# The second MoE product of units 4 to 7 as seven half products

## The chip, the cores and the metric

One Trainium2 chip, one of its cores. The metric is the device time of one execution in microseconds; each kernel's time is the median of several executions. TensorE (PE) multiplies and loads weights (PEld), VectorE (DVE), ScalarE (ACT) and GpSimd (POOL) compute on tiles, and SyncE (SP) issues most transfers.

## The reference, cut to what matters

```python
# attention: batch 4, 8 heads, sequence 768, head dimension 64
k_sum = k.reshape(B, H, nb, 32, D).max(axis=3); v_sum = v.reshape(B, H, nb, 32, D).mean(axis=3)
scores = concat(where(|i - j| < 16, q k^T / sqrt(D), -1e9), q k_sum^T / sqrt(D) + log(32))
a = softmax(scores); attn = a @ concat(v, v_sum)
x = attn.transpose(0, 2, 1, 3).reshape(3072, 512)
# MoE
h = x @ w_in          # 3072 x 512 by 512 x 2048
g = h - tanh(h)
y = g @ w_out         # 3072 x 2048 by 2048 x 512
```

## The kernel before

The 3072 tokens are cut into eight units of 384 (half a sequence each), the 2048 hidden columns into 16 slices f of 128. For a unit the attention gives x transposed; a slice of the first product ("in") gives 128 hidden columns x 384 tokens in a PSUM bank; three ScalarE passes and one multiplication turn it into g (`moe_act_small`); the second product ("out", `moe_out`) adds g of that slice times a slice of `w_out` to three banks of 128 tokens x 512 columns, `pY0` to `pY2`.

To keep fp32 accuracy in a fast format every operand is split into a high and a low part, and a product is three matmuls: high x high, high x low, low x high. Those parts of g are made by `moe_split` (tiles gh and gl).

Units 2 to 7 are taken in pairs (2,3), (4,5), (6,7): their first product is already done as seven products of halves instead of eight (`moe_in_seven`). It needs sums of quarters of `w_in`, which `make_sums` computes once and stores in device memory (`scr`, 16 and more stores); `load_sums` brings them back for each pair into one of three buffers `wraw`. A group g of 0 to 7 gives four g-tiles: slices g and g + 8 of both units. `x_operands` makes the sums of the x quarters. The second product of all units is the plain one; `store_y` scales a bank into an SBUF tile on ScalarE and stores it.

Nothing is emitted as it is written: `do`, `either` and `dma` add tasks to a plan, with what they read and write. Then `follow` walks the written list `ORDER` of all 3628 tasks and emits them so; `ON` has a letter per task that picks the engine where there is a choice (D, A, P for VectorE, ScalarE, GpSimd, S for SP's queue, T for TensorE), `FILL` the number of small matmuls on the identity that are put ahead of a task to keep the clock up. So the order on each engine and on each queue is fixed by these lists. All instructions bear line 56, that of the helper that emits them, so groups are told apart by their tiles' names.

At the end `seen`, the largest sum of squares of h, decides whether a second, general version of the program runs; with these inputs it does not.

Of the kernel before, what the change touches and what calls it, by code (L numbers as in the profile page):

```python
# [21 lines left out]
RAWB = 3  # L22
# [7 lines left out]


FILL = {125: 18, 154: 12, 158: 2, 190: 14, 188: 6, 286: 2}
ON = 'PPAPAPPDDPPPPSSSSAASADSSSSDASSSDDASSSSSSSSSSSSSSSSASSDASASDSAASDDDSSSSSSSSSSSSDDDDSADDDSDDDDSDDDDSADDDSDDDDSADDDSADDDTAAAASSSTADDASSSTDDDDDDAAAAAADDDAAAPATATATATADDDDDDAAAAAAPDAAADAATDTATDTATDDDDDDAAAAAADDADAADPTATDTATADDDDDDAAAAAADDDADDDATATATATATTTTADAAAPSASSDTTTTDDAAAPSSSSSSSSSSSSSSTDDDDDDAAAAAADDDAPADATATATATADDDDDDDAAAAAADDPPAAAATATATATADTTTADTADAAAPSSSSTAAAATTTADTADAAAPSSSSDSSSSDDASSSSDSSSSDTTTADSDDDDTADAAAPSASSDTTTADSADDDTADAAAPAPSSSSSSSSSSSSSSTDDDDDDAAAAAADDAAADAPTATATATADDDDDDDAAAAAADDAADAAATATATATADSADDDAPTTTSDDDDTADAAADAPSSSSTAAAASADDDADTTTSADDDTADAAADADSADDDADTTTSADDDTADAAADADSADDDADTTTSADDDTADAAADADSADDDADTTTSADDDTADAAADADSADDDADTTTSADDDTADAAADAPSSSSSSSSSSSSSSTDDDDDDAAAAAAPDDDDDAAAAAATATATATADDDDDDAAAAAADDDDDDADAAAATATATATASADDDADTTTSADDDTADAAAPADSDDDDADTTTSDDDDTADAAADADSDDDDADTTTSADDDTADAAADADSADDDADTTTSADDDTADAAAPADSDDDDADTTTTAAADDDSSSSSSSSSSSSSSTDDDDDDAAAAAADDPDDDAAADAPTATATATADDDDDDAAAAAADDDDDDAAAAAATATATATASDDDDADTTTASASASTAAADADSSSSDSSSSDDASSSSDSSSSDTTTTAAADADSPSPSPSPTTTTAAADAPTTTTAAADAPTTTTAAADSSSSDDDDDDADSADSADSSSSSSSSSSSSSSTDDDDDDAAAAAAPDDDDDAAAAAATATATATADDDDDDAAAAAADDDDDDAAAAAATATATATATTTTAAADSSSSDDDDDPADSADSADTATTTTAAADSSSSDDPDDDADSADSADTTTTAAADSSSSDDDDDDADSADSAPTTTTAAADSSSSDDDDDDADSADSADSSSSSSSSSSSSSSTDDDDDDAAAAAADDPDDDAAAAAATATATDTADDDDDDAAAAAADDDDDDAAAAAATATATATATTTTAAADSSSSDDDDDDADSADSADTTTTAAADSSSSDDDDDDADSADSADSPSPSPSPTTTTAAADSSSSDDDDDDADSADSADTTTTAAADADTTTTAAADADTTTTAAADADTASSSSDSSSSDDPSSSSDSSSSDTTTADADADADADADDDDDDDDDADADADADADAPADADSSSTTADTATTADSTATDAAADADTTTASASAAAAADDPTTTSSSTTDDTATTDDSTATDAAADDPSSSSSSSSSSSSSSTDDDDDDAAAAAADDDDDDDDADAPTDTATDTDDDDDDDAAAAAADDPDDDDAPPAPTATDTDTATTTAAADDPTTTSSSTTADTDTTADSTDTDAAAPADTTTAAADADTTTSSSTTDDTDTTDDSTATDAAADADTTTAAAPDPTTTSSSTTDDTDTTDDSTATDAAADADTTTAAADDPSSSSSSSSSSSSSSTDDDDDDAAAAAADDDDDDDDPPAATDTDTATADDDDDDAAAAAADDPDDDAPDDDPTATATDTDTTTSSSTTDDTATTADSTDTDAAADAPSSSSDSSSSDDASSSSDSSSSDTTTAAADDDSPSPSPSPTTTSSSTTDDTDTTADSTATDAAADDDTTTAAAPDDTTTSSSTTDDTATTDDSTATDAAADDDTTTAAADDPTATTTAAADDDTTTASAAASAAADDDSSSSSSSSSSSSSSTDDDDDDAAAAAADDDDPDPPDPDPTATATATADDDDDDAAAAAADDDDDDDAPDADTDTDTDTDTTTAAADDDTTTAAAPDDTTTAAADDDTTTAAADDDTTTAAADADTTTAAADADTTTAAADDPSSSSSSSSSSSSSSTDDDDDDAAAAAADDDDDDDPDDDPTATDTATDDDDDDDAAAAAAPDDDDDAAPPAPTATATDTATTTAAADADSPSPSPSPTTTAAADADTTTAAADAPTTTAAADDDTTTAAADADTATTTAAADDPTTTAAADADSSSSDSSSSDDDSSSSDSSSSDTTTDPAPAPADADADPDDPDDDDADADDDDDADADDDADSSSTTADTATTADSTATDAAAPADTTTASAAASAAAPAPTTTSSSTTADTDTTADSTDTDAAADDDSSSSSSSSSSSSSSTDDDDDDAAAAAAPDDDDDDAPDPPTATDTATADDDDDDAAAAAAPDDDDDDPPAPPTATDTDTATTTAAAPAPTTTSSSTTDDTDTTADSTATDAAAPAPTTTAAAPDDTTTSSSTTDDTATTADSTATDAAADAPTTTAAADDDTTTSSSTTADTATTADSTDTDAAAPDPTTTAAAPDPSSSSSSSSSSSSSSTDDDDDDAAAAAADDDDPDPPADDATATATDTADDDDDDAAAAAAPDDDPDPDADPATDTDTDTDTTTSSSTTDDTDTTADSTATDAAAPAPSSSSDSSSSDDASSSSDSSSSDTTTAAADDDTTTSSSTTADTDTTADSTDTDAAAPADTTTAAAPDDTTTSSSTTDDTATTADSTATDAAAPDDTTTAAADAPTTTAAAPDDTTTASASASAAAPDDSSSSSSSSSSSSSSTDDDDDDAAAAAADDDDPDDDAPPPTDTDTATDDDDDDDAAAAAAPDDDDDAPDAAPTATATATATTTAAADDDTTTAAADDPTTTAAADAPTTTAAAPADTTTAAADDDTTTAAAPDDTTTAAAPDDSSSSSSSSSSSSSSTDDDDDDAAAAAADDPDDDPAPAADTDTDTATADDDDDDAAAAAADDDDDDDPDAPATDTATATATTTAAAPDDTTTAAADDPTTTAAAPDDTTTAAADADTTTAAADDDTTTAAADADTTTAAAPDDTTTADAPDDADADADDDDDPDDDADDDDDDPADADADADSSSTTDDTATTADSTDTDAAAPADTTTASASAAAAADAPTTTSSSTTDDTATTADSTDTDAAAPDPTTTAAADAPTTTSSSTTADTDTTDDSTATDAAADDDTTTAAADADTTTSSSTTDDTATTDDSTATDAAAPAPTTTAAADADTTTSSSTTDDTDTTDDSTDTDAAAPADTTTAAAPDDTTTSSSTTDDTATTADSTDTDAAADDDTTTAAADADTTTSSSTTADTDTTDDSTDTDAAAPAPTTTAAADAPTTTSSSTTADTDTTADSTATDAAAPDDTTTAAADDPTTTAAAPDDTTTASAAAAAAADDDTTTAAADADTTTAAADDDTTTAAADDDTTTAAADDDTTTAAADDDTTTAAADDDTTTAAADDPTTTAAADDDTTTAAADDDTTTAAADDDTTTAAADDPTTTAAAPAPTTTAAADDDTTTAAADDDTTTDDTTTAAASAASADTD'


SIGNED = set()

SLACK = 2.0

EITHER_QUEUE = {"y store"}
# [4 lines left out]
class Engine:  # L48


    def __init__(self, tc, engine):
        self._tc, self._engine = tc, engine

    def __getattr__(self, name):
        op = getattr(self._engine, name)
        return lambda *args, **kwargs: self._tc.keep_in_program_order(op(*args, **kwargs))  # L56


class Task:
    __slots__ = ("issue", "ahead", "index", "costs", "go", "after", "order", "level", "count", "ready", "next", "start", "engine", "cost", "place", "out", "banks", "behind", "moves", "kind", "name")  # L60

HELD = {"w shift", "w low", "w sign", "w low part", "w low part 2", "w high part", "w high part 2", "w scale", "normal", "g high", "g low", "g", "cube", "big", "top pre", "k move", "sum guard", "s whole", "s mix", "s high", "s low", "x mix", "x high", "x low"}
# [24 lines left out]
class Plan:  # L89
# [20 lines left out]
    def add(self, kind, costs, go, r=(), w=()):  # L110
# [15 lines left out]
        for base in dict.fromkeys(key[0] for key in (*r, *w)):  # L126
# [15 lines left out]
            self.touch.setdefault(base, []).append(t)  # L142
        t.after.discard(t)
        t.order.discard(t)
        t.order -= t.after
        return t

    def follow(self, idle):

        tasks = [self.tasks[n] for n in ORDER]  # L150
        free = dict.fromkeys((PE, DVE, ACT, POOL, SP), 0.65)
        dma, held, left = 0.0, {DVE: 0.0, POOL: 0.0}, 0.0
        clock, used, seen, done = Clock(), {}, {}, []
        spot, rest, lanes = 0, self.fill, [0.0] * 8
        for t in tasks:
            e = next(iter(t.costs)) if len(t.costs) == 1 else {"D": DVE, "A": ACT, "P": POOL, "S": SP}[ON[t.index]]
            assert all(a in seen for a in (*t.after, *t.order)), t.name
            t.engine, t.cost = e, t.costs[e]
            now = max([free[e]] + [seen[a] for a in t.after] + [at for b in t.banks for a, at in used.get(b, {}).items() if a != e])
            if e == PE:  # L160
                cost, go = idle
                if now > free[PE]:
                    free[PE] = max(free[PE], min(now, seen.get(self.tasks[0], now)))
                if spot == 1:
                    free[PE] = max([free[PE]] + [min(now, at) for a, at in used.get(rest[3], {}).items() if a != PE])
                for _ in range(FILL.get(t.index, 0) if FILL is not None else int(0.7 * (now - free[PE]) / cost) if spot < 2 and now - free[PE] > 0.4 else 0):
# [11 lines left out]
                if t.kind in ("in", "out", "p turn"):  # L178
# [12 lines left out]
            if SP in t.costs:  # L191
                t.out = free[e] = now + t.issue
                t.moves = max(dma, now + t.ahead)
                dma = t.moves + t.cost
                seen[t] = dma + self.SEEN[SP]
                lanes.append(seen[t])
# [141 lines left out]
def program(  # L338
# [652 lines left out]
    def gu(u, f):  # L991
        return (lambda: at(("gu", u, f))), [(("gu", u, f), 0)]
# [348 lines left out]
```

## Time and profile before

| | |
|---|---|
| median of 3 runs | 658.32 us (656.73 to 660.75) |
| the profiled execution | 663.1 us, of which the span of instructions 661.4 us |
| mean granted clock of TensorE | 0.995 |
| busy: TensorE, weight loads | 632.8, 532.5 us |
| busy: VectorE, ScalarE, GpSimd | 447.7, 453.3, 151.2 us |
| moved by DMA | 113.24 MB |

Busy shares are means over the whole span. What bounds a stage is read from that stage: the windows give busy time of each engine per stretch, the chain of waits what ended last. Matmul records are pipelined: the record of one is longer than the time from its start to the next one's, so the cost of a matmul in a stream is the distance of starts, which a merged row of many gives best. A weight load has its own record beside the matmul before it.

### The profile page before, as it was taken

What the parts mean: (1) busy time and instruction counts of PE and PEld (TensorE: products, weight loads), DVE (VectorE), ACT (ScalarE), POOL (GpSimd) and SP (SyncE); (2) the same over time, 40 slices, a digit from 0 to 9 for tenths busy, and PEclk for the clock granted to TensorE, in tenths of its full rate; (3) what the DMA queues carried; (4) which work ended last, traced back from release to release, by engine and by line L of the source; (5) the groups of instructions that cost most, each with busy time, mean ns of one, the idle gap of its engine ahead of it and who ended that gap; (6) DMA issues with size and microseconds to landing.
All of it is one profiled execution on the core that took longest, in us unless ns stands there. A gap on an engine that the chain in (4) does not pass through costs nothing.

```text
span 661.4 us, 15115 instructions
## 1 busy us (share of the span) xinstructions
PE 632.8 (96%) x5297; PEld 532.5 (81%) x5297; DVE 447.7 (68%) x1285; ACT 453.3 (69%) x1371; POOL 151.2 (23%) x240
## 2 busy tenths in 40 slices
PE   5779989999899999999999999999999999999997
PEld 4746557778779888989888789989888799999885
DVE  2778999996998884655778874455766944334472
ACT  3578899989798863545689873644789853433773
POOL 2002310103301410113524421313343211112101
PEclk9899999999999999999999999999999999999999
DMA  7678887746687686667453465655443155444001
GB/s 201 158 212 241 230 238 223 240 146 188 209 282 259 210 266 174 194 211 219 135 156 82 115 184 178 207 163 175 136 130 84 59 173 191 146 166 153 33 17 66
DMA packets 120736, 113.24 MB, mean 171 GB/s; under 512 B 45008, under 2 KB 88528, under 8 KB 120656
## 3 DMA queue, kind: packets, MB, share of 16 engines
q1 hardware_dynamic: 117216, 109.19, 54.3%
q10 hardware_dynamic: 3440, 3.05, 1.4%
q8 instruction: 43, 0.70, 0.5%
q14 instruction: 37, 0.30, 0.2%
HBM read 88.87 MB, written 20.97 MB: 166 GB/s over the span
## 4 chain that ended last, share of the span: by engine, by line
PE 72%; DMA 12%; DVE 6%; ACT 4%; SPq 3%; issue 2%; DVEq 0%; ACTq 0%
PE pY L56 34%; PE pH L56 31%; PE pS L56 4%; DMA wraw<-in_moe_w_in_dram 3%; PE pX L56 3%; DMA raw<-in_k_dram 3%; SPq L56 3%; ACT prob L56 2%; DMA raw<-in_q_dram 1%; DMA scr<-wraw 1%; DMA wraw<-in_moe_w_out_dram 1%; DVE tmp L56 1%; DVE prob L56 1%; DVE kT L56 1%; DVE wraw L56 1%
## 5 line engine op out<-in xcount | busy, mean ns | idle before, releaser
L56 ACT ACTIVATE prob<-prob,stat 128x120 f32<-128x120 f32 x294 | 107.8, 386 | 35.4 <-DVE stat L56 34.8
L56 PE MATMUL pY<-wl,gh 128*128 128x512 f32 x288 | 113.4, 394 | 0.2 <-DVE wl L56 0.2
L56 PE MATMUL pH<-wf,wraw 128*128 128x384 f32 x552 | 112.1, 338 | 1.3 <-ACT gu L56 1.2
L56 PEld LDWEIGHTS pH<-wf,wraw 128*128 128x128 f32 x552 | 97.4, 188 | 7.1 <-ACT gu L56 1.6
L56 PE MATMUL pH<-wg,wraw 128*128 128x384 f32 x432 | 84.0, 337 | 0.2
L56 PE MATMUL pY<-wh,gh 128*128 128x512 f32 x204 | 83.2, 408 | 0.0
L56 PE MATMUL pY<-wh,gl 128*128 128x512 f32 x204 | 80.7, 396 | 0.0
L56 PEld LDWEIGHTS pH<-wg,wraw 128*128 128x128 f32 x432 | 75.9, 188 | 3.8 <-DMA wraw<-scr 0.5
L56 PE MATMUL pY<-wg,gh 128*128 128x512 f32 x168 | 68.6, 408 | 0.0
L56 ACT ACTIVATE gu<-gu 128x384 f32<-128x384 f32 x128 | 65.8, 520 | 1.9
L56 PE MATMUL pY<-wg,gl 128*128 128x512 f32 x168 | 66.5, 396 | 0.4 <-DVE gl L56 0.4
L56 PE MATMUL pH<-o,wf 128*128 128x384 f32 x188 | 65.5, 445 | 0.0
L56 POOL TENSOR_TENSOR gl<-gu,gh 128x384 fp32r<-128x384 f32 x28 | 29.5, 1055 | 144.3 <-ACT gh L56 64.1
L56 PEld LDWEIGHTS pY<-wl,gh 128*128 128x128 f32 x288 | 54.2, 188 | 9.1 <-DVE wl L56 0.6
L56 ACT ACTIVATE gv<-pH 128x384 f32<-128x384 f32 x37 | 18.1, 489 | 45.3 <-PE pH L56 45.1
L56 PEld LDWEIGHTS pH<-o,wf 128*128 128x128 f32 x188 | 34.9, 191 | 14.8 <-issue 0.9
L56 PEld LDWEIGHTS pY<-wh,gl 128*128 128x128 f32 x204 | 38.2, 187 | 8.9 <-DVE gl L56 0.4
L56 PE MATMUL pY<-wf,gh 128*128 128x512 f32 x108 | 44.5, 439 | 0.0
L56 PEld LDWEIGHTS pY<-wh,gh 128*128 128x128 f32 x204 | 38.3, 188 | 7.0 <-issue 0.5
L56 POOL TENSOR_TENSOR gu<-gu,gt 128x384 f32<-128x384 f32 x25 | 25.7, 1030 | 79.8 <-ACT gu L56 69.9
L56 ACT ACTIVATE gt<-gu 128x384 f32<-128x384 f32 x48 | 24.9, 519 | 26.9 <-DVE gu L56 25.9
L56 POOL TENSOR_TENSOR prob<-prob,stat 128x120 f32<-128x120 f32 x45 | 18.5, 415 | 89.3 <-DVE stat L56 80.3
(210 smaller groups left out, 1382.5 us busy)
## 6 DMA issues: line engine op xcount, KB each, us to landing
wraw<-scr SPq DMA_DIRECT2D x72, 512.0 KB
wraw<-in_moe_w_in_dram SPq DMA_DIRECT2D x16, 512.0 KB
wraw<-in_moe_w_out_dram SPq DMA_DIRECT2D x16, 512.0 KB
scr<-wraw SPq DMA_DIRECT2D x16, 512.0 KB
wraw<-scr SPq DMA_DIRECT2D x24, 256.0 KB
raw<-in_q_dram SPq DMA_DIRECT2D x54, 96.0 KB
vw<-in_v_dram SPq DMA_DIRECT2D x60, 80.0 KB
raw<-in_k_dram SPq DMA_DIRECT2D x48, 96.0 KB
```

Of the source, the lines that this page charges most:

```text
L56: return lambda *args, **kwargs: self._tc.keep_in_program_order(op(*args, **kwargs))
```

## The change

For the pairs (4,5) and (6,7) the second product is also done as seven products of halves (`OUT7 = (4, 6)`). Units 2 and 3 and the unpaired units 0 and 1 stay as they were.

- `make_out_sums`, called eight times in the time of units 2 and 3, forms four differences of quarters of `w_out`, splits them into parts and stores them, and a plain quarter, in device memory (`scr2`).
- `moe_out_seven` does the seven products for a pair. Each runs over eight f; for each f it makes high and low parts of the left operand (some of them sums of g-tiles, "h mix", written over the g-tiles), and for three token tiles three matmuls of 256 columns. Two token tiles share a bank. Five products take their right side from `scr2`: four loads of 512 KB each into the three `wraw` buffers, one for two f. The results are joined in SBUF and stored as halves of 256 columns, 12 stores of 128 KB per pair.
- All 32 g-tiles of a pair must be kept until then; they get buffers of weights and attention operands that are no longer needed (`late_g`, `done_w`), for which some fixed tiles become ring tiles.
- In `moe_in_seven` the last two products change places, and odd groups of the last pair use banks `pX` and `pS1`. The last small load has its own buffer `ts`.
- Loads of v of batch 0 and mean copies of units 0 and 1 may be issued by GpSimd.
- `ORDER` (now 4152 tasks), `ON` and `FILL` are new throughout. Read against the tasks, they say: on TensorE the seven products of units 4 and 5 come nearly all before the first products of units 6 and 7, those are followed by the seven products of units 6 and 7, and with them only six attention tasks are left. In the last seven products 40 of 56 low parts, 25 of 32 mixes and 13 of 56 high parts are VectorE's, 16 low parts and 7 mixes GpSimd's, 43 high parts ScalarE's; in the first two of them VectorE has 15 low parts, 17 mixes and 5 high parts, GpSimd one low part and 7 mixes. Eleven transfers in the early part have GpSimd's letter. `FILL` sums to 54 small matmuls before and 48 now.

```diff
+OUT7 = (4, 6)
...
+            elif SP in t.costs and e == POOL:
+                now = max(now, others.pop(0), held[DVE])
+                t.issue, t.ahead, held[POOL] = 0.62, 1.8, now + 0.62
...
+    def seven_out(u):
+        return small_only and u - u % 2 in OUT7
...
+        made[SCR2] = spool.tile([5, FH, P, 2 * DH], F32, name="scr2")
...
+    def make_out_sums(g):
+        ia, ib = 2 * g + 1, 2 * (g + FH) + 1
+        ts = t0, t1 = [buf(("to", g, n), "tmp", [P, DM], F32, TMPS) for n in range(2)]
+        for hl in range(2):
+            dma("o store", ...)
+        for t, i in zip(ts, (ia, ib)):
+            either("o whole", ...)
...
+        mix(b11, b12, b11)
+        mix(b12, b22, b12)
+        mix(b22, b22, b11)
+        mix(b21, b21, b22)
+        for h, t in enumerate(ts):
+            hi = buf(("ts", g, h), "ts", [P, DM], F32R)
...
+            either("o high", ...)
+            either("o low", ...)
+            keep(0, lambda hi=hi: at(hi), (hi, 0))
+            keep(1, lambda t=t: at(t), (t, 0))
...
-                        dma("v load", ..., w=[(vw, (n, part))])
+                        dma("v load", ..., w=[(vw, (n, part))], any_queue=b == 0)
...
+        tags = ("pX", "pS1") if u == NU - 2 and g % 2 else ("pH", "pH")
+        z, y = (bank((n, u, g), tag) for n, tag in zip(("z", "yx"), tags))
...
+        product(5, "B22", y, False)
+        join(y, c12, k12, s2)
         load_sums(u, g, 3)
         product(6, "T4", z, False)
-        part(c21, k21)
-        product(5, "B22", y, False)
-        join(c12, k12, s2)
+        part(z, c21, k21)
...
+    def moe_out_seven(u):
...
+            def right(f):
+                h = f // 2
+                if h not in tiles:
+                    st = tiles[h] = buf(("tx", u, t, h), "wraw", [P, 2, 2, DH], F32R, RAWB)
+                    dma("o load", ...)
...
+        def product(left, right, before=None):
+            m = turn_of[0] = turn_of[0] + 1
+            held.update({0: bank(("m", u, m, 0), f"pY{m % 2}"), 1: bank(("m", u, m, 1), "pY2")})
+            for f in range(FH):
+                x, xk = before(f) if before else left[f]
+                n = count[0] = count[0] + 1
+                gh, gl = (buf(("g2", u, n, hl), (("gh", "gl"), ("gt", "gv"))[n % 2 if n > FH else 0][hl], [P, U], F32R, 2) for hl in range(2))
+                either("h high", {ACT: 0.42, DVE: 0.29}, ...)
+                either("h low", {POOL: 0.975, DVE: 0.48}, ...)
+                (high, low), wk_ = right(f)
+                for i in range(NT):
+                    ps, c = place(i)
+                    def go(i=i, ps=ps, c=c, gh=gh, gl=gl, high=high, low=low, f=f):
+                        o, s = at(ps)[:, c:c + DH], slice(P * i, P * (i + 1))
+                        tensor.matmul(o, at(gh)[:, s], high(), start=f == 0 and c == 0, stop=False, skip_group_check=c > 0)
+                        tensor.matmul(o, at(gh)[:, s], low(), start=False, stop=False, skip_group_check=c > 0)
+                        tensor.matmul(o, at(gl)[:, s], high(), start=False, stop=f == FH - 1, skip_group_check=c > 0)
+                    do("out half", PE, 0.35, go, r=[(gh, 0), (gl, 0), *wk_], w=[(ps, c)])
...
+        product(a11, summed(4))
+        snap("s1")
+        def first(f):
+            s1 = buf(("s1", u, f), "gu", [P, U], F32, RINGS["gu"])
+            s1 = (lambda: at(("s1", u, f))), [(("s1", u, f), 0)]
+            mix(ALU.add, s1, a21[f], a22[f])
+            mix(ALU.subtract, a21[f], a11[f], a21[f])
+            mix(ALU.subtract, a11[f], s1, a11[f])
+            return s1
+        product(None, summed(0), first)
+        snap("s5")
+        product(a11, summed(3))
+        join("s1", "u2")
+        plus("u4", "u2", "s5")
...
+        product(None, whole(FH, 1), fourth)
+        join("u4")
+        store("u4", 0, 1)
+        product(a21, summed(1))
+        join("u2", "u3")
+        plus("s5", "u3", "s5")
+        store("s5", 1, 1)
+        product(a12, whole(FH, 0))
+        join("s1")
+        store("s1", 0, 0)
+        product(a22, summed(2))
+        join("u3")
+        store("u3", 1, 0)
...
+            if small_only and m == (6, 0) and 4 in OUT7:
+                moe_out_seven(4)
...
+            if small_only and OUT7 and j >= 36 and (j - 36) % 3 == 0 and (j - 36) // 3 < FH:
+                make_out_sums((j - 36) // 3)
...
         do("seen max", DVE, ...)
+        moe_out_seven(NU - 2)
```

## Rows read from the trace of the kernel before

**Rows 1.** The page's first part: busy us (share of the span) xinstructions.
```profile
PE 632.8 (96%) x5297; PEld 532.5 (81%) x5297; DVE 447.7 (68%) x1285; ACT 453.3 (69%) x1371; POOL 151.2 (23%) x240
```
**Rows 2.** The page's chain that ended last, by engine.
```profile
PE 72%; DMA 12%; DVE 6%; ACT 4%; SPq 3%; issue 2%; DVEq 0%; ACTq 0%
```
**Rows 3.** Busy time by stage of the whole span.
```profile
core 0: us, PE busy (x) PEld busy (x) DVE busy (x) ACT busy (x) POOL busy (x), PEclk, DMA share, GB/s
0.00:240.00 240.00, 217.90 (x2192) 168.12 (x2193) 198.36 (x573) 191.56 (x607) 44.73 (x88) 0.99 0.73 218
240.00:380.00 140.00, 138.04 (x1217) 120.13 (x1217) 96.35 (x302) 91.59 (x289) 42.73 (x71) 1.00 0.57 168
380.00:440.00 60.00, 59.98 (x479) 54.69 (x481) 33.96 (x90) 32.27 (x94) 13.45 (x19) 1.00 0.60 185
440.00:540.00 100.00, 100.00 (x857) 85.91 (x847) 67.63 (x219) 76.33 (x232) 32.48 (x45) 1.00 0.41 125
540.00:640.00 100.00, 100.00 (x503) 90.37 (x503) 43.42 (x85) 51.26 (x129) 14.69 (x15) 1.00 0.37 127
640.00:661.40 21.40, 16.88 (x74) 13.30 (x72) 8.02 (x20) 10.33 (x26) 3.17 (x3) 0.99 0.14 51
```
**Rows 4.** The chain in order of time, two pieces: start us, us, what.
```profile
600.81 3.14 PE pH L56 x18
...
624.85 31.93 PE pY L56 x138
```
**Rows 5.** The page's group of weight loads of first products: busy, mean ns.
```profile
L56 PEld LDWEIGHTS pH<-wf,wraw 128*128 128x128 f32 x552 | 97.4, 188 | 7.1 <-ACT gu L56 1.6
```
**Rows 6.** Timeline of TensorE at 30 us, small matmuls at full clock: start, us.
```profile
29.81 1.84 PE L56 MATMUL pY<-ident 128*128 128x128 f32 x15
```
**Rows 7.** Loads for tile pY, 12.8 to 14.2 us: duration ns min/median/max.
```profile
L56 PEld LDWEIGHTS pY<-ident x14: 192/192/192, 12.7 to 14.2; 128*128 128x128 f32 x14
```
**Rows 8.** Timeline of ScalarE in the last stage.
```profile
637.69 0.53 ACT L56 ACTIVATE gt<-o 128x384 f32<-128x384 f32 x1 [2.58 <-DVE o L56]
638.12 0.51 ACT L56 ACTIVATE o<-o 128x384 f32<-128x384 f32 x1
...
638.63 0.51 ACT L56 ACTIVATE o<-o 128x384 f32<-128x384 f32 x1
...
639.13 0.92 ACT L56 ACTIVATE o<-o 128x384 f32<-128x384 f32 x2
```
**Rows 9.** The page's GB/s in 40 equal slices.
```profile
GB/s 201 158 212 241 230 238 223 240 146 188 209 282 259 210 266 174 194 211 219 135 156 82 115 184 178 207 163 175 136 130 84 59 173 191 146 166 153 33 17 66
```
**Rows 10.** The chain in order of time at 228 us.
```profile
227.85 4.28 DMA wraw<-scr
```
**Rows 11.** Timeline of VectorE and GpSimd in the last stage.
```profile
636.00 0.55 DVE L56 TENSOR_TENSOR o<-pH,gv 128x384 f32<-128x384 f32 x1
636.23 1.01 POOL L56 TENSOR_TENSOR gl<-wh,gh 128x384 fp32r<-128x384 f32 x1 [16.14 <-DVE gh L56]
636.47 1.19 DVE L56 TENSOR_TENSOR o<-o,gt 128x384 f32<-128x384 f32 x1
...
637.79 0.36 DVE L56 CAST gh<-o 128x384 fp32r<-128x384 f32 x1
...
638.25 0.56 DVE L56 TENSOR_TENSOR gl<-o,gh 128x384 fp32r<-128x384 f32 x1
```
**Rows 12.** Timeline of SP's queue in the early part.
```profile
26.86 6.06 SPq L56 DMA_DIRECT2D vw<-in_v_dram  x5
```
**Rows 13.** Waits of TensorE to 240 us: us, times, longest.
```profile
PE pH L56 <- DMA gt<-in_v_dram: 6.7, 2, 4.0
```
**Rows 14.** VectorE's instructions on tile kT.
```profile
L56 DVE STREAM_TRANSPOSE kT<-raw x12: 952/972/981, 57.5 to 454.3; 128x768 f32<-128x768 f32 x12
```
**Rows 15.** Timeline of the end.
```profile
656.12 1.34 ACT L56 ACTIVATE wraw<-pY 128x512 f32<-128x512 f32 x3 [0.81 <-PE pY L56]
...
656.37 0.40 PE L56 MATMUL pY<-wh,gl 128*128 128x512 f32 x1
...
657.49 0.34 ACTq L56 DMA_DIRECT2D out_dram<-wraw  x1
```

More of the change, by code (lines that the diff above doesn't have):

```diff
@@ L60 @@
     __slots__ = ("issue", "ahead", "index", "costs", "go", "after", "order", "level", "count", "ready", "next", "start", "engine", "cost", "place", "out", "banks", "behind", "moves", "kind", "name")
-HELD = {"w shift", "w low", "w sign", "w low part", "w low part 2", "w high part", "w high part 2", "w scale", "normal", "g high", "g low", "g", "cube", "big", "top pre", "k move", "sum guard", "s whole", "s mix", "s high", "s low", "x mix", "x high", "x low"}
+HELD = {"w shift", "w low", "w sign", "w low part", "w low part 2", "w high part", "w high part 2", "w scale", "normal", "g high", "g low", "g", "cube", "big", "top pre", "k move", "sum guard", "s whole", "s mix", "s high", "s low", "x mix", "x high", "x low", "h mix", "h high", "h low", "o whole", "o mix", "o high", "o low"}
 class Clock:
@@ L153, in follow @@
         clock, used, seen, done = Clock(), {}, {}, []
-        spot, rest, lanes = 0, self.fill, [0.0] * 8
+        spot, rest, lanes, others = 0, self.fill, [0.0] * 8, [0.0] * 8
         for t in tasks:
@@ L177, in follow @@
                 now = max(now, free[PE])
-                if t.kind in ("in", "out", "p turn"):
+                if t.kind in ("in", "out", "out half", "p turn"):
                     t.cost, left = t.cost + max(left, 0.0), -1.0
@@ L195, in follow @@
                 seen[t] = dma + self.SEEN[SP]
-                lanes.append(seen[t])
+                (others if e == POOL else lanes).append(seen[t])
             else:
@@ L453, in copy, with dma @@
             e.tensor_scalar(out, x, scale, None, op0=ALU.mult)
-    def dma(kind, go, nbytes, run, r=(), w=(), both=False):
-        fixed_part, rate = {"w load": (0.0, 260e3), "s load": (0.3, 330e3), "s store": (0.05, 390e3), "chunk load": (0.0, 230e3), "mean put": (0.1, 300e3), "y store": (0.0, 320e3)}.get(
+    def dma(kind, go, nbytes, run, r=(), w=(), both=False, any_queue=False):
+        fixed_part, rate = {"w load": (0.0, 260e3), "s load": (0.3, 330e3), "s store": (0.05, 390e3), "o load": (0.3, 330e3), "o store": (0.05, 390e3), "chunk load": (0.0, 230e3), "mean put": (0.1, 300e3), "y store": (0.0, 320e3)}.get(
             kind, (0.04, 270e3) if run < 1024 else (0.0, 330e3))
@@ L461, in dma @@
             t = plan.add(kind, {SP: cost, ACT: cost}, go, r, w)
+        elif small_only and any_queue:
+            t = plan.add(kind, {SP: cost, POOL: cost}, go, r, w)
         else:
@@ L541, in program @@
         else:
-            fixed(("wl", i), [P, DM], F32R)
+            buf(("wl", i), f"wl{i}", [P, DM], F32R)
         if i not in group_of:
@@ L1274, in program @@
                 convert(2 * m2[1] + 1)
-            moe_out(*m2)
-            if m2[1] == order_of(m2[0])[-1]:
+            if not seven_out(m2[0]):
+                moe_out(*m2)
+            if not seven_out(m2[0]) and m2[1] == order_of(m2[0])[-1]:
                 for i in range(NT):
@@ L1289, in program @@
                 moe_in_seven(*m)
-            moe_act(*m)
+                if seven_out(m[0]):
+                    for n in range(4):
+                        moe_act(m[0] + n % 2, m[1] + FH * (n // 2))
+            if not seven_out(m[0]):
+                moe_act(*m)
             if small_only and m[0] == 1 and 5 <= m[1] < FH + 5:
                 make_sums(m[1] - 5)
-        if m1 is not None and not (m1[0] == 0 and m1[1] in WHOLE_F):
+            if small_only and OUT7 and j >= 36 and (j - 36) % 3 == 0 and (j - 36) // 3 < FH:
+                make_out_sums((j - 36) // 3)
+        if m1 is not None and not (m1[0] == 0 and m1[1] in WHOLE_F) and not seven_out(m1[0]):
             moe_split(*m1)
```

117 lines of the change are left out of this document (95 added, 22 removed).

## The prediction

> **What bounds the kernel now.** I read the page's busy times first, then its chain of waits, then busy time by stage, and last the spacing of instructions inside one stage. TensorE is busy 632.8 of 661.4 us [rows 1], and 72% of the chain that ended last is its work [rows 2]. By stage [rows 3] it idles 22.1 us before 240 us, where VectorE is busy 198 and ScalarE 192 us and DMA's share is 0.73; 2.0 us up to 380; nothing at all from 440 to 640; the 4.5 us in the last row are the drain of the stores. So from 240 us on the time is the number of matmuls times their spacing, at full granted clock (1.00, the 2.4 GHz level). Beside it VectorE idles 44 of 140 us from 240 to 380 and 57 of 100 from 540 to 640, ScalarE about as much. A change that takes columns from TensorE there is worth what it takes, as long as the others keep up.
>
> **TensorE's own sum.** For a pair of units the old second product is 2 units x 16 slices x 3 token tiles x 3 passes = 288 matmuls of 512 columns. The new one is 7 products x 8 slices x 3 x 3 = 504 matmuls of 256, 7/8 of the columns. Two pairs: 576 become 1008. The spacing of the old ones is 31.93 / 138 = 0.2314 us; that of 384 columns is 3.14 / 18 = 0.1744 us [rows 4]. No matmul of 256 columns of this kind is in the trace. A straight line through the two gives 0.1174, in proportion to 512 it is 0.1157; I take 0.117. Old: 576 x 0.2314 = 133.3 us; new: 1008 x 0.117 = 117.9; **15.4 us less**, with 14.9 (0.1174) and 16.7 (0.1157) as near ends.
>
> Far ends: each matmul loads its own weights, and a load's record lasts 188 ns [rows 5]. If half of a matmul no longer hid its load, spacing could go to 0.188 us: 1008 x 0.188 = 189.5, 56 us more than before. Against it stand the matmuls on the identity that keep the clock up: 15 of them, each with its own load of 128 columns, take 1.84 us, that is (1.84 - 0.27) / 14 = 0.112 us from one to the next [rows 6], while the record of such a load lasts 192 ns [rows 7]; so loads overlap what is around them. That is the nearest row (same load, no long stream over it), and 0.112 is under 0.117 by only 4%. The Trainium skill (TensorE: Matmul & The Clock Gate, "LDWEIGHTS (loading the stationary operand)" and "Back-to-back issue gap") puts a load at columns / 1.2, an estimate of 107 ns here, and the gap of a matmul at N / 2.4 + 2.5, an estimate of 109 ns at 256 columns; by that the new work were 110 us and the saving 23. The trace disagrees with the same formula at the sizes it has: 0.1744 against 162.5 ns, 0.2314 against 215.8 ns. I keep the rows.
>
> **The last stage.** In the new order TensorE does the products of units 4 and 5 first, then the 56 first products of units 6 and 7 (336 x 0.1744 = 58.6 us), then their 168 tasks of half products (504 x 0.117 = 59 us), with six other tasks in 118 us. Before, the two kinds were mixed in this stretch, so what feeds each is used more densely now.
> - ScalarE in the first 58.6 us: 32 slices of three activations. Five in a row last from 637.69 to 640.05, 0.47 us each with the reading of sums [rows 8]; 32 x 3 x 0.47 = 45 us. It fits.
> - Loads of the stored sums for the first products: 24 of 512 KB and 8 of 256 KB are 14.7 MB in 58.6 us, 251 GB/s; the trace moved 282 in its best slice and 127 in the stage 540 to 640 [rows 9, 3]. A buffer has 5 x 1.05 = 5.2 us between its last and its next use; a load of 512 KB took 4.28 us from issue to landing [rows 10]. It fits, narrowly.
> - Loads for the half products: one tile serves two slices, 18 x 0.117 = 2.1 us; with three buffers a load has 4.2 us. Against 4.28 [rows 10] this is even. In the first three products of units 6 and 7, all of stored sums, 12 tiles follow each other; a load longer by 1 us costs (5.28 + 2.1 - 6.3) / 3 = 0.36 us a tile, 4 us.
> - Vector work in the first two half products: the lists give 15 low parts, 17 mixes and 5 high parts to VectorE, 8 such operations to GpSimd. At 0.56, 0.56 and 0.36 us [rows 11] VectorE needs 15 x 0.56 + 17 x 0.56 + 5 x 0.36 = 19.7 us, GpSimd 8 x 1.01 = 8.1 [rows 11], and the two don't run together: beside the GpSimd operation at 636.23 a VectorE one of two SBUF operands took 1.19 us instead of 0.56 [rows 11]. Together 27.8 us, against 48 tasks x 3 x 0.117 = 16.8 of TensorE. What may be done ahead is held by the three buffers for S1 and two pairs for the parts: some 6 mixes and 2 low parts, 4.5 us, more where TensorE still works on first products. That leaves 0 to 6.5 us of waiting.
> I take 1.5 us for all of this (nearest row: the stage 540 to 640, no idle time at all [rows 3], but with less vector work); bounds 0 and 8.
>
> **The second weights' sums.** Eight groups of two wholes (some 0.7 us each on VectorE, 512 columns to the 384 of [rows 11]), four mixes of 256 columns (0.4), two high and two low parts: some 5 us a group, 40 us in all over VectorE, GpSimd and ScalarE, spread over the stage 240 to 380 and later, where VectorE alone idles 44 us [rows 3]. Their stores are 8 x 1.31 = 10.5 MB, 37 us of DMA at the 282 GB/s of the best slice [rows 9]; DMA's share there is 0.57 [rows 3], which leaves 60 us. Cost nothing; if this cover is gone, the first products of units 2 to 5 wait for their loads behind the stores on SP's queue, up to 5 us. The reordering of products within a slice (the last join earlier) and the other PSUM banks in odd groups cost nothing: no matmul is added.
>
> **Early part and end.** Eleven loads and mean copies of the first batch go from SP's to GpSimd's queue, and the order of everything is new. SP issues without a break there (five loads took 6.06 us to issue) and TensorE waits 6.7 us for loads of v [rows 12, 13]; so eleven issues fewer on SP, some 0.45 us each, could give up to 5 us. The trace has no transfer issued by GpSimd. What it may lose is bounded by VectorE instructions in the way: the longest common one there, the 0.97 us transpose [rows 14], for each of eleven is 11 us. I take 0 (the nearest row, SP's own issues, speaks for a gain, VectorE's load against it), -5 to +11 for the range. The Trainium skill (SBUF — State Buffer, "SBUF: two separate sides") warns of just this: while VectorE holds the shared port, GpSimd cannot write descriptors, and a transfer of 620 ns took 3100; by its figures eleven transfers were late by an estimate of 27 us together. No run here shows it yet; it is rival four below.
>
> The end is even: before, the last matmul at 656.37 is followed by two ScalarE halves until 657.46, a store issued at 657.49 and 3.9 us to the end [rows 15]; now by one VectorE join of 256 columns and a store of the same 128 KB. The check of the maximum now also comes last on TensorE, off the stores' way.
>
> Sum against the profiled execution, 661.4 us of span and 663.1 with what lies around it: 663.1 - 15.4 + 1.5 = 649.2. That execution is 4.8 us above the median of the three runs, 658.32; so I forecast 658.3 - 13.9 = **644.5 us**.
>
> **Rivals.**
> 1. The last stage is not fed. Vector work and three load buffers make TensorE wait, 6.5 us in the two first half products and 1 to 3 in the other loads, and the same once more, smaller, for units 4 and 5, where attention can step in: 644.5 - 1.5 + 8 to 11 = 651 to 654. For it: 27.8 us of work beside 16.8. Against it: ScalarE takes most high parts, and the order starts mixes during the first products. Chance 0.17.
> 2. The early part gains from the new queue and order: 644.5 - 5 - 2 = 636 to 639. For it: 22 us of TensorE's idle time lie there [rows 3]. Against it: VectorE, ScalarE and DMA are all near full in that stage, and nothing is taken from them. Chance 0.09.
> 3. Slower: weight loads set the pace. From a spacing of 133.3 / 1008 = 0.132 us on, the change loses; at the 0.1744 of the 384-column matmuls, which would mean that a fixed time and not columns decides, 1008 x 0.1744 = 175.8, 42.5 us more: 701 us; at 0.145, 671. Against it: [rows 6, 7]. Chance 0.05.
> 4. GpSimd's transfers wait for VectorE: 11 us by the rows make 655; twice that, when each also holds up what is behind it on GpSimd's queue, 666. Against it: only eleven, and TensorE has other work by 60 us. Chance 0.05.
> 5. The saving in columns is there but the new order as a whole stalls earlier stages (units 2 to 5 with 32 MB more to move), 10 us: 655 to 660. Chance 0.06.
> That the seven products do not happen can be ruled out by counting the loops.
>
> **How the numbers follow.** Forecast 0.58 with its own range 639 to 651 (the near ends of the spacing, 0 to 8 us of waiting, and half of what the early part may gain); 1% of 658.3, about what a measurement of this kernel can tell from no change, is 6.6 us: faster means below 651.7, slower above 664.9. Faster: 0.58 + 0.09 + a third of rival 1 and some of the rest, 0.06 + 0.03 = 0.76. Same: the rest of rival 1, 0.11, and 0.05 of rivals 4 and 5 = 0.16. Slower: 0.05 + 0.03 = 0.08. The range from 637 takes in rival 2, and up to 655 rival 1 and the row-bound of rival 4; outside are rivals 3 and 5 and half of 4.
>
> **What would show it.** Half matmuls 0.115 to 0.119 us apart in runs inside one product (over 0.13: rival 3). TensorE without idle time from the end of the first product of units 6 and 7 on, above all in the second half product; idle time there with VectorE or GpSimd named is rival 1, with a load of the sums named its other half. TensorE idle 22 us before 240 us; 10 more with loads of v named is rival 4, 5 fewer rival 2. The span of the changed kernel should be some 14 us shorter, nearly all of it after 440 us. Wrong would be a saving that comes before 240 us, or half matmuls at 0.117 and a time that has not fallen.

## The result, and the profile after

The change makes the kernel slower by just under 1%: 667.56 us median (19 runs) against 660.75 for the kernel before (19 runs beside them), ratio 1.0093, 95% interval [1.0071, 1.0116]. 644.5 us, 2.1% faster, was forecast. Ratios and intervals compare fast executions only, so they differ a little from the quotient of the medians (1.0103 here).

The page of the changed kernel, busy us first (answers [rows 1]), then the chain by engine (answers [rows 2]; it could be followed back over a third of the span only, so its shares are of little use here):

```profile
PE 626.9 (94%) x5717; PEld 540.5 (81%) x5717; DVE 531.2 (80%) x1427; ACT 487.9 (73%) x1461; POOL 213.5 (32%) x300
...
PE 23%; DMA 3%; DVE 3%; ACT 1%; issue 1%; POOL 0%; ACTq 0%; DVEq 0%
```

TensorE has 5.9 us less busy time than before; VectorE has 83 more, ScalarE 35, GpSimd 62. The same stages as [rows 3]:

```profile
0.00:240.00 240.00, 218.73 (x2189) 165.29 (x2190) 205.94 (x582) 188.10 (x599) 54.64 (x103) 1.00 0.78 225
240.00:380.00 140.00, 133.14 (x1157) 113.06 (x1155) 104.87 (x306) 102.93 (x322) 53.88 (x79) 1.00 0.70 218
380.00:440.00 60.00, 58.26 (x547) 52.14 (x546) 46.57 (x121) 48.24 (x143) 21.16 (x27) 1.00 0.72 225
440.00:540.00 100.00, 98.10 (x1001) 93.35 (x1000) 86.51 (x249) 70.83 (x215) 32.94 (x42) 1.00 0.67 213
540.00:640.00 100.00, 97.42 (x654) 95.83 (x655) 74.68 (x145) 73.01 (x178) 40.68 (x40) 1.00 0.62 214
640.00:665.90 25.90, 21.28 (x177) 20.80 (x176) 12.62 (x28) 4.74 (x9) 10.17 (x10) 0.96 0.47 157
```

Up to 240 us TensorE idles 21.3 us, as before. From 240 to 640 it idled 2.0 us of 400 in the kernel before; now it idles 13.1. No single wait is to blame; waits of TensorE in two stretches, 320 to 440 and 440 to 560 us (us in all, times, longest), where the kernel before has 0.6 us in one wait and none:

```profile
PE pS L58 <- ACT probT L58: 1.5, 1, 1.5
PE pY L58 <- ACT gh L58: 1.1, 2, 0.8
PE pH L58 <- DMA wraw<-scr: 1.0, 2, 0.8
PE pH L58 <- DVE qT L58: 1.0, 1, 1.0
...
PE pH L58 <- DVE wh L58: 1.1, 1, 1.1
PE pY L58 <- DMA wraw<-scr: 0.8, 1, 0.8
PE pH L58 <- DVE vw L58: 0.7, 1, 0.7
PE pH L58 <- ACT gv L58: 0.6, 1, 0.6
```

Busy shares hide part of it, because the records of pipelined matmuls overlap. So I also took the time from the start of each matmul to the start of the next, less its spacing (0.174, 0.231, 0.118 us for 384, 512, 256 columns), and added up what is over 0.03 us. (How the small matmuls of attention are taken moves the result a little: other ways of counting give 16 to 19 us more.) Such gaps are 52.7 us in the kernel before and 70.6 after, 17.9 more: 0.7 fewer up to 320 us, 9.5 more from 320 to 440, 2.1 from 440 to 520, 4.7 from 520 to 560, 2.3 behind that. Less 13.4 us for the columns (1008 matmuls of 256 instead of 576 of 512), that is the 4.5 us between the two spans, more closely than such a count can promise.

The chain in order of time in the last stage (answers [rows 4]), and three half matmuls from a timeline of TensorE:

```profile
603.41 3.50 DMA wraw<-scr
...
610.88 4.29 DMA wraw<-scr
...
615.31 39.27 PE pY L58 x324
...
654.60 4.23 DMA wraw<-scr
```

```profile
633.16 0.28 PE L58 MATMUL pY<-wg,gt 128*128 128x256 f32 x1
633.28 0.28 PE L58 MATMUL pY<-wl,gt 128*128 128x256 f32 x1
633.40 0.28 PE L58 MATMUL pY<-wg,gv 128*128 128x256 f32 x1
```

Half matmuls start 0.12 us apart (mean 0.1189 over all that no gap follows; 39.27 / 324 = 0.1212 with the small gaps). The last stage is fed: three loads on its chain, but only 0.6 us of waiting for them.

### The profile page after: what moved, and what is told of

It reads as the page before. It is cut to its first block, busy times and chain, and to the rows that moved or that the text cites. A ratio compares the mean times of both kernels' runs of the same rounds, so it can differ in the third digit from the quotient of the medians.

```text
span 665.9 us, 16626 instructions
## 1 busy us (share of the span) xinstructions
PE 626.9 (94%) x5717; PEld 540.5 (81%) x5717; DVE 531.2 (80%) x1427; ACT 487.9 (73%) x1461; POOL 213.5 (32%) x300
## 5 line engine op out<-in xcount | busy, mean ns | idle before, releaser
L58 PE MATMUL pY<-wl,gh 128*128 128x512 f32 (+1 forms) x192 | 70.5, 367 | 0.0
L58 POOL TENSOR_TENSOR tmp<-tmp 128x256 f32<-128x256 f32 (+3 forms) x61 | 37.7, 619 | 62.7 <-DMA tmp<-in_v_dram 41.3
L58 PE MATMUL pY<-wraw,gh 128*128 128x256 f32 x288 | 54.2, 283 | 0.0
L58 PE MATMUL pY<-wg,gh 128*128 128x512 f32 (+1 forms) x120 | 45.5, 380 | 0.6 <-ACT gh L58 0.6
L58 PE MATMUL pY<-wh,gh 128*128 128x512 f32 (+1 forms) x108 | 43.8, 405 | 1.4 <-ACT gh L58 0.8
L58 PEld LDWEIGHTS pY<-wraw,gh 128*128 128x128 f32 x288 | 44.5, 189 | 0.1
L58 PE MATMUL pY<-wg,gl 128*128 128x512 f32 (+1 forms) x120 | 43.7, 364 | 0.7 <-DVE gl L58 0.7
L58 PE MATMUL pY<-wh,gl 128*128 128x512 f32 (+1 forms) x108 | 41.7, 386 | 0.3 <-DVE gl L58 0.2
L58 PE MATMUL pY<-wraw,gl 128*128 128x256 f32 x144 | 40.9, 284 | 0.2
L58 PE MATMUL pY<-wraw,gt 128*128 128x256 f32 x192 | 38.0, 290 | 1.5 <-DMA wraw<-scr 1.3
```

## The experiments

**Theory and rivals.** Theory: the vector work that the change adds crowds VectorE, ScalarE and GpSimd between 250 and 560 us, and TensorE waits in small pieces. Rivals: the 32 MB more of transfers; the new order by itself; half products that cost more than they save. Ratios are to the kernel before, run beside each group; the changed kernel stands at 1.0093 from its own group. A difference of two such ratios is uncertain by some 0.0035, 2 us, and more for runs of few executions.

**1. The sums' arithmetic, and the stores.** In `make_out_sums`:

```
-  either("o whole", ..., lambda e, t=t, i=i: e.tensor_tensor(...), ...)
+  either("o whole", ..., lambda *_: None, ...)      # o mix, o high, o low alike
```

The stores keep their places and bytes, and write parts of the weights as they are.

> The changed kernel without the arithmetic of the second weights' sums (no whole, mix, high and low parts; the stores keep their places and bytes but write the weights' own parts, so the output is not the reference's). Compared with the changed kernel's 667.6 us. Crowding theory (the added work of VectorE, ScalarE and GpSimd between 250 and 560 us is what TensorE waits for): the sums are about a third of that work, so 5 to 8 us of the 16 us of new gaps go, 660 to 663 us. DMA theory (the 32 MB more are what it waits for): no change, 666 to 668. Order theory (the new order as a whole fits the chip worse than the old one): no change, 666 to 668.

Measured: 662.36 us, 1.0007 [0.9981, 1.0032]. And with `dma("o store", lambda e: None, ...)` too, while the half products load as many bytes of the first weights' stored sums:

> As the run without the sums' arithmetic, and without the 10.5 MB of stores too (the loads of the half products read the first weights' stored sums instead, as many bytes). Crowding theory: as without the arithmetic, 659 to 663 us. DMA theory: the stores lie on SP's queue ahead of the loads of units 2 to 5; with them gone 5 to 10 us come back, 658 to 662, and nearly all of it against the run that still stores. Order theory: 665 to 668.

Measured: 662.6 us, 1.0003 [0.998, 1.0025]. The arithmetic of the sums is worth 0.0086 x 661 = 5.7 us, as crowding expects; the stores are worth nothing that shows. From 320 to 380 us TensorE idles 4.5 us in the changed kernel and 1.3 without the arithmetic, where VectorE then has 11 us less to do:

```profile
320.00:380.00 60.00, 55.46 (x537) 43.16 (x535) 53.94 (x166) 53.71 (x172) 16.92 (x27) 1.00 0.61 188
```

```profile
320.00:380.00 60.00, 58.73 (x583) 47.00 (x582) 42.47 (x147) 55.08 (x177) 11.84 (x21) 1.00 0.66 199
```

The sums' instructions from 240 to 380 us in the changed kernel (tile ts; duration ns min/median/max, first and last start) show the price and how GpSimd lengthens it: 1267 ns for a low part at 326.35 us, beside GpSimd's subtraction there, where the median takes 693.

```profile
L58 DVE TENSOR_TENSOR tmp<-tmp,ts x13: 678/693/1267, 281.0 to 363.0; 128x512 fp32r<-128x512 f32 x13
L58 ACT ACTIVATE ts<-tmp x9: 613/631/634, 258.9 to 358.4; 128x512 fp32r<-128x512 f32 x9
L58 DVE CAST ts<-tmp x7: 419/428/762, 277.1 to 362.6; 128x512 fp32r<-128x512 f32 x7
L58 POOL TENSOR_TENSOR tmp<-tmp,ts x3: 1285/1293/1297, 266.9 to 290.6; 128x512 fp32r<-128x512 f32 x3
```

**2. Plain second products in the new order.** In both places `moe_out_seven(u)` becomes a plain product in the same task slots, matmuls of 512 columns in some, nothing in the others. A task whose inputs now come later than its place in ORDER is emitted as soon as they are there, so the order is not quite the same.

```
-                moe_out_seven(4)
+                moe_out_plain(4)
...
-        moe_out_seven(NU - 2)
+        moe_out_plain(NU - 2)
```

> The changed kernel in the same order and with the sums made and stored, but with the second product of the last two pairs plain again, 576 matmuls of 512 columns for 1008 of 256 (eight slices of weights stand in for sixteen, the mixes and the loads of stored sums are left out; the output is not the reference's). By the spacings TensorE has 133.3 - 122.2 = 11 us more to do. Crowding theory: 11 us more of matmuls, 5 to 8 us fewer gaps because 51 mixes and a quarter of the splits are gone: 669 to 674 us. Order theory: 11 us more, gaps as in the changed kernel: 676 to 680. If the half products themselves cost more than they save (waits inside them): under 664.

Measured: 694.84 us, 1.0502 [1.0486, 1.0519]. And without the sums and their stores:

> The changed kernel's order, queues and banks with plain second products and without making or storing the sums: what is left of the change is the order itself, eleven transfers on GpSimd's queue, the join moved within a slice and the other banks in odd groups (output as in the run without half products, not the reference's). Crowding theory: as the kernel before, 658 to 663 us, since the added work is gone. DMA theory: the same. Order theory: 672 to 678, the 16 us of gaps still there on top of the old number of columns.

Measured: 689.8 us, 1.0404 [1.0385, 1.0422]. Both are far above every expectation, and I had put plain matmuls only into the slots of four half products. So later the same with the 32 steps spread over all slots of a pair:

> What is left of the change when the sums (arithmetic and stores), mixes and loads are out and the second products of the last two pairs are plain again, this time with their 32 steps a pair spread evenly over the places of the 56 steps of half products, so that the order keeps its density (eight weight slices stand in for sixteen; the output is not the reference's). TensorE has the columns of the kernel before, VectorE and ScalarE the work of the kernel before. If the new order and its engine assignment cost time by themselves: the bare run with fewer splits (658.7) plus the 11 to 13 us of columns, 669 to 672. If the half products' own small gaps are what holds the bare run up: 660 to 664, as the kernel before.

Measured: 688.96 us, 1.0432 [1.0401, 1.0464], above what was expected too. Busy time of this run by stretch at the start of the last stage:

```profile
520.00:540.00 20.00, 19.23 (x246) 15.34 (x242) 13.02 (x52) 12.11 (x45) 6.72 (x9) 1.00 0.41 117
540.00:560.00 20.00, 13.79 (x53) 11.21 (x50) 11.01 (x22) 7.23 (x17) 2.98 (x3) 0.60 0.31 105
560.00:580.00 20.00, 19.18 (x107) 18.86 (x107) 10.32 (x19) 14.33 (x38) 7.10 (x7) 0.97 0.67 218
```

From 540 to 560 us TensorE idles and its granted clock falls to a mean of 0.60, between its levels of 2.4 and 1.2 GHz. This is a seam: units 4 and 5 are done, attention has just ended, and the first products of unit 6 wait for their operands with nothing beside them. My gaps there are 15.5 us from 520 to 560 in this run (the lower clock included), 5.3 in the changed kernel, 0.6 before. So these three runs don't give the price of the order by itself, since taking the half products out opens the seam wider. They show only that in this order half products are the faster of the two: the plain ones without sums take 26 us more than the half products without sums, not the 11 to 13 of the columns. One thing they do show of the order: in the evenly spread run, which has plain products and none of the added work, TensorE idles 3.9 us from 320 to 440 us, against 0.6 in the kernel before.

**3. Mixes, loads and splits.** The mixes out (`mix` issues nothing), the loads out (`summed` gives resident slices, `return whole(FH, t % 2)(f)`), or all, with the splits that the change adds.

> The changed kernel without the sums and differences of activations ahead of the half products (the mixes; the products then work on other operands, so the output is not the reference's). 65 instructions fewer, 52 of them VectorE's at some 0.56 us, all between 457 and 661 us. Against the changed kernel's 667.6 us. Crowding theory: 4 of the 9 us of gaps after 440 us go, 662 to 665. If only the sums' arithmetic was in the way: 666 to 668.

Measured: 668.41 us, 1.0135 [1.0081, 1.0188]. Nothing comes back.

> The changed kernel in its own order without the 40 loads of the second weights' stored sums, 20 MB (the half products take resident weight slices; the output is not the reference's); the sums are still made and stored, the mixes are there. From the run without sums and stores (662.6) to the bare run (657.3) mixes and loads together gave 5 us, and the mixes alone nothing. Loads theory: 662 to 664, the 5 us are the loads'. Crowding theory: 666 to 668, the mixes cost only once the sums are out of the way.

Measured: 665.38 us, 1.0068 [1.0044, 1.0093]: 1.7 us, inside the two intervals. Unclear.

> The changed kernel without the sums' arithmetic and stores and without the loads of stored sums, but with the mixes (the half products take resident weight slices; the output is not the reference's). Without sums and stores it took 662.6 us, without mixes and loads too 657.3. Crowding theory: the mixes hold 3 of these 5 us, 660 to 662. Loads theory: 657 to 659.

Measured: 657.0 us, 0.9935 [0.9911, 0.9959]. With the sums out of the way the loads cost (1.0003 - 0.9935) x 661 = 4.5 us.

> The changed kernel with its 1008 half matmuls and their splits, but without the sums' arithmetic, their stores, the mixes and the loads of stored sums (the half products take resident weight slices; the output is not the reference's). What was added beside TensorE is gone but for 48 splits. The run without sums and stores stands at 662.6 us. Crowding theory: 653 to 657, since the mixes take their gaps with them and the saving in columns (13 us by the measured 0.119 us) shows for the greater part. If the half products themselves or the order hold the time: 660 to 663. If the loads of stored sums were the hidden price: the same as under crowding here, but not in the run that leaves out mixes alone.

Measured: 657.33 us, 0.9948 [0.9918, 0.9979].

> As the bare run, and the second to fourth half products of each pair use the split operands that the first left, so that the 48 splits that the change adds are gone (32 a pair as in the kernel before). Now only TensorE's work differs from the kernel before, in the new order. Crowding theory: 648 to 653, close to the kernel before less 13 us. If half products or order hold the time: within 2 us of the bare run.

Measured: 658.67 us, 0.9962 [0.9935, 0.9989]. Mixes and added splits cost nothing that shows. The crowding theory holds for the sums, and falls for the half products' own vector work: there loads were the price. How the two share it depends on which goes first: loads alone give 1.7 us, and the sums behind them 8.8; together they give (1.0093 - 0.9935) x 661 = 10.4 us. With nearly all of the added work gone the kernel gains 2.5 to 4.3 us of 13; the rest is not crowding by added work.

**4. The early transfers.** In the list of engines the eleven go from GpSimd (P) back to SP (S); then the other way in the kernel before, in its own order:

```
+        elif small_only and any_queue:
+            t = plan.add(kind, {SP: cost, POOL: cost}, go, r, w)
...
+  dma("v load", ..., any_queue=b == 0)      # ON: P for eleven tasks
```

> The changed kernel, whole, with the eleven early transfers of the first batch back on SP's queue in the same order. Crowding theory: the early part is not where the time went, 666 to 669. If GpSimd's queue delays the start (rival four): 658 to 664. If it had helped: 670 to 675.

Measured: 673.16 us, 1.0181 [1.0134, 1.0227].

> The kernel before, whole, in its own order, with the eleven early transfers (loads of v and copies of means of the first batch) issued by GpSimd instead of SP: that one part of the change alone. In the changed kernel the move back cost 5.6 us. If the queue itself is worth it: 655 to 659, faster than both kernels. If the changed order was only laid out around it: 660 to 664. Rival four of the prediction (transfers wait while VectorE works): 665 to 672.

Measured: 658.75 us, 0.9956 [0.9938, 0.9974]: faster than both kernels. On SP the transfers cost the changed kernel 0.0088 x 661 = 5.8 us; moved alone they gain 2.9. The first 40 us, in turn before, before with GpSimd's queue, changed, changed with SP's queue:

```profile
0.00:40.00 40.00, 27.38 (x457) 24.27 (x458) 22.18 (x72) 20.09 (x79) 5.70 (x31) 0.96 0.70 180
```

```profile
0.00:40.00 40.00, 28.30 (x470) 23.80 (x470) 25.60 (x90) 23.34 (x94) 12.13 (x41) 1.00 0.84 217
```

```profile
0.00:40.00 40.00, 28.26 (x475) 23.45 (x476) 25.89 (x92) 22.32 (x89) 12.48 (x43) 1.00 0.88 205
```

```profile
0.00:40.00 40.00, 26.64 (x450) 22.48 (x451) 24.33 (x87) 20.55 (x82) 6.73 (x33) 1.00 0.75 184
```

With the second queue DMA's share there is 0.84 to 0.88 instead of 0.70 to 0.75, and VectorE and ScalarE have 1.6 to 3.4 us more done.

**5. Laid out again.** Whole kernels with another ORDER and ON and nothing else (some 350 tasks change engine), found by moving tasks one by one in the list's own model with durations from the traces.

> The changed kernel, whole: same tasks, buffers and arithmetic, only the order of issue and the engine of tasks that may run on two are laid out again, with mean durations read from the two traces (for example 0.457 us where the list has 0.29 for a high part on VectorE, 0.119 us for a half matmul, means of low parts and wholes that include GpSimd's hold on VectorE, 0.05 us more from an end to its waiter) in place of the list's prices. Order theory (the list was laid out so tightly for its low prices that on the chip the added vector work makes it slip, +13 us between 240 and 630 us): 643 to 657 us, 10 to 24 less than the changed kernel. Crowding as such (the work does not fit whatever the order): 664 to 668. Late loads: 662 to 668, since no transfer gets shorter.

Measured: 668.0 us, 1.01 [1.0049, 1.0151].

> The kernel before, whole, laid out again in the same manner with the same durations. If the slip of the changed kernel is its own, because only its engines are full: 655 to 661, little to gain, and the relaid changed kernel is the faster of the two by up to 10 us. If every order for the low prices slips: 641 to 655, and then the comparison of the two relaid kernels tells what the change itself is worth: by columns 13 us for the changed one, by the durations the order was laid out with 2 us against it.

Measured: 665.1 us, 1.0035 [1.0009, 1.0061]. The theory of low prices is not borne out: it expected up to 25 and 19 us less, and neither kernel is shorter at all. One layout of each doesn't rule it out. What that model doesn't see shows in the relaid changed kernel, waits from 240 to 320 us, where it laid the loads of sums too tight:

```profile
PE pH L58 <- DMA wraw<-scr: 5.4, 4, 2.9
```

**6. The old engines.** 105 letters of ON between 320 and 440 us as in the kernel before.

> The run without the sums' arithmetic and stores, with 105 tasks between 320 and 440 us (normalizations of attention, copies out of PSUM, gating products, parts) put on the engine that they have in the kernel before; among them 26 normalizations go from ScalarE back to GpSimd (14) and VectorE (12). Without sums it took 662.6 us with 8.7 us of gaps from 320 to 440 us, 5 more than before, and ScalarE was busy 55.6 of 60 us there. If these gaps come from the lists making room for the sums: 3 to 5 us back, 658 to 660. If the order, not the engines, holds them: 662 to 665.

Measured: 666.75 us, 1.0085 [1.0056, 1.0113].

> The run without sums, stores and loads of stored sums (657.0), with the same 105 tasks on their engines of before. If the gaps from 320 to 440 us come from the engine lists: 653 to 655. If the order holds them: 657 to 660.

Measured: 661.19 us, 1.0001 [0.9979, 1.0024]. Both are 4 to 5 us slower than with the new lists, and slower than either theory expected. These letters are not the cause; they help.

**What is left.** The run without sums and loads by stretch: 320 to 440, and 520 to 560 us, of the kernel before, the changed one, and that run:

```profile
320.00:440.00 120.00, 119.40 (x1065) 103.15 (x1067) 81.31 (x240) 82.05 (x249) 40.62 (x65) 1.00 0.49 146
520.00:560.00 40.00, 40.00 (x247) 36.33 (x246) 21.24 (x46) 24.61 (x61) 6.68 (x7) 1.00 0.41 134
```

```profile
320.00:440.00 120.00, 113.72 (x1082) 95.29 (x1081) 100.51 (x286) 101.96 (x313) 38.07 (x54) 1.00 0.66 207
520.00:560.00 40.00, 37.44 (x400) 34.90 (x400) 33.35 (x95) 32.05 (x99) 20.09 (x23) 1.00 0.59 194
```

```profile
320.00:440.00 120.00, 116.96 (x1110) 100.40 (x1108) 87.01 (x262) 103.27 (x323) 34.90 (x50) 1.00 0.55 168
520.00:560.00 40.00, 37.35 (x326) 35.68 (x312) 31.61 (x86) 32.05 (x96) 16.88 (x19) 1.00 0.63 197
```

ScalarE has 21 us more than before in the first stretch even with the sums gone, and the second stretch is no better than in the changed kernel. The instructions on tile pY (second products and halves) alone, 420 to 460 and 540 to 600 us, before and after, suggest a reason:

```profile
420.00:460.00 40.00, 15.05 (x58) 10.61 (x59) 0.00 (x0) 0.00 (x0) 1.00 0.61 189
...
540.00:600.00 60.00, 22.68 (x89) 16.33 (x89) 0.00 (x0) 1.66 (x3) 1.00 0.48 164
```

```profile
420.00:460.00 40.00, 2.59 (x9) 1.77 (x10) 0.00 (x0) 1.74 (x3) 1.00 0.73 238
...
540.00:600.00 60.00, 2.08 (x18) 2.25 (x18) 0.83 (x2) 0.00 (x0) 1.00 0.68 239
```

Each of the seven half products runs over all eight groups of a pair, and the banks hold one or two products at a time, so at most the first can run beside the pair's own first products. Before, second products filled 15 and 23 us of these stretches; now first products, with their activations, stand there nearly by themselves. But rows of 20 us of the changed kernel bear this out only in part:

```profile
340.00:360.00 20.00, 16.81 (x184) 12.21 (x183) 18.91 (x68) 18.68 (x65) 2.92 (x5) 1.00 0.61 188
420.00:440.00 20.00, 20.00 (x241) 18.75 (x240) 15.56 (x42) 17.79 (x55) 8.12 (x11) 1.00 0.72 231
540.00:560.00 20.00, 17.98 (x100) 17.32 (x101) 15.15 (x27) 15.73 (x41) 9.36 (x9) 1.00 0.58 203
560.00:580.00 20.00, 20.00 (x117) 20.00 (x116) 13.50 (x27) 16.91 (x45) 12.09 (x13) 1.00 0.73 254
```

In the middle of such stretches, from 420 to 440 and from 560 to 580 us, TensorE does not idle. It idles 2.0 us at the seam, from 540 to 560, and most of all from 340 to 360 us, where second products still stand beside (tile pY has 25.6 us from 320 to 360, and had 27.2 before). So the lost mixing can explain the seam; what holds TensorE from 340 to 420 us is not shown; the waits named there are of 1.5 us at most, and several are for tiles of attention (probT, qT). In the run without sums and loads the gaps beyond those of the kernel before lie about half from 320 to 440 us and half from 520 to 560 (some 4.8 and 3.9 us, attention's matmuls taken at their median spacing). Part of them is the half products' own: from 440 us on, gaps behind half matmuls are 4.5 us in that run, and those behind plain ones 2.2 in the kernel before. No run shows the price of any of these alone.

## Why the prediction was wrong, point by point

By medians and ratios, in us of 661: 13.4 saved in columns; 10.4 lost to the sums and the loads together (5.7 to the sums' arithmetic and 4.5 to the loads when the sums go first); and about 9 put down to the new order, because the run without sums and loads stands at -4.3 and not at -13.4. The measured loss is 0.0093 x 661 = 6.1. The 9 us are a remainder and no measurement of their own: they hold whatever else is new in order, engine lists, buffers and banks, and the eleven early transfers too. What supports them is the trace of that run, with 62.0 us of gaps against 52.7.

- **TensorE's own sum** (-15.4): the mechanism was right, the size a little large. The measured 0.1189 gives 133.3 - 119.9 = 13.4 us. That lies outside the near ends that I gave, and far from the far end; rival three falls. The Trainium skill (TensorE: Matmul & The Clock Gate, "Back-to-back issue gap") gives its formula, an estimate of 0.109 us here, for an isolated matmul, and about 131 ns at 512 columns for a stream with weight loads; the trace, with 0.1189 and 0.2314 us, bears out neither. The half matmuls at the forecast distance and a time that has not fallen are what the prediction itself named as a sign of being wrong. (The prediction's last sum, 658.3 - 13.9, gives 644.4, not 644.5.)
- **The last stage** (+1.5): right; 2.3 us of gaps from 560 us on, 0.6 of them with loads named. Rival one falls. But the sentence that what feeds each kind "is used more densely now" was priced there alone. It holds for units 4 and 5 from 320 us on and for the seam at 540 too, and there it cost.
- **The second weights' sums: "Cost nothing"** is the first step that failed. They cost 5.7 us, and not as the text had it for lost cover, through stores on SP's queue (these cost nothing that shows), but through the vector work. That was also more than the 40 us of the text: without it the three engines are busy 54 us less (VectorE 25.8, GpSimd 22.6, ScalarE 6.0). The cover was a mean: 44 idle us of VectorE from 240 to 380 us. The last sums lie at 320 to 363 us, beside attention, where VectorE is busy 17 to 19 of every 20 us now. Stage means hide it.
- **Loads of the sums**: called a narrow fit and, for the half products, even in the last stage, and nothing elsewhere. They cost 4.5 us once the sums are away.
- **The order** is the step that was missing from the sum. Rival five named just this, a saving that is there while the new order stalls units 2 to 5, with 10 us and a chance of 0.06. That its size fits the remainder is luck: it put the stall down to the 32 MB more to move, and the 9 us are what stays when stores and loads are gone; the sums and the loads come on top. The order had been given no row of its own: that at most one half product can run beside its own pair's first products, and what that does to the mix of work from 320 us on, could be read from the diff and from [rows 3], whose idle time of 0.0 from 440 to 640 us stood over a stretch with both kinds mixed.
- **Early part** (0): as forecast in sum, 21.3 us of idle time for 22.1, but the queue itself does what rival two said: 5.8 us of loss when undone, 2.9 of gain by itself. This gain is inside the 9 us of the order, so what else is new there costs more than 9. Rival four falls. The Trainium skill (SBUF — State Buffer, "SBUF: two separate sides") has GpSimd's descriptors wait for VectorE's hold on the port. The eleven transfers landed 3.2 to 5.2 us after issue, with medians of 4.3 to 4.9; what they take with VectorE at rest no run shows, so the trace tells neither that they waited nor that they didn't. The kernel gained all the same.

```profile
vw<-in_v_dram POOLq DMA_DIRECT2D x4, 80.0 KB, 4.3
vw<-mean POOLq DMA_DIRECT2D x2, 48.0 KB, 4.8
```

What stays open is what in the new order holds TensorE from 340 to 420 us, and whether another order of the same tasks is free of the 9 us: one other layout of order and engines was no faster, and the old engines made them larger.

## What to carry to other kernels

An algorithm that takes columns from a saturated engine can also take away the freedom to interleave them (here that fits the seam; its price was not isolated): ask of each product what it must wait for and what it stood beside, before you count its columns. Price added vector work in the 20 us in which it lies and not by the idle time of a stage. The smallest part of a change, here a second queue for eleven early transfers, can be the part worth keeping, so run it alone.

## What the runs showed that I had not expected

A pause can cost TensorE a little more than itself: behind a wait for a load at 658.96 us the second half matmul starts some 0.19 us after the first, not 0.12 (two take 0.48 us where two in a stream take 0.40). In the changed kernel 39 of the 53 gaps behind half matmuls are of this size, 0.07 to 0.11 us. But only 10 of them stand at the start of a stream after such a pause; 17 come where half matmuls follow small ones of attention, and the other 12 with neither ahead of them. So a pause is not the whole of it, and no run tests why.

```profile
658.29 0.40 PE L58 MATMUL pY<-wraw,gh 128*128 128x256 f32 x2
658.53 0.28 PE L58 MATMUL pY<-wraw,gl 128*128 128x256 f32 x1
658.96 0.48 PE L58 MATMUL pY<-wraw,gt 128*128 128x256 f32 x2 [0.15 <-DMA wraw<-scr]
```
